# Masks of ones and zeros only: a bias product without its correction, w_in converted behind it, and a new order of the experts' blocks

## The chip, the cores and the metric

One Trainium2 chip, one of its cores. The metric is device time in microseconds (us); lower is better. The engines are TensorE (PE, with PEld for its weight loads), VectorE (DVE), ScalarE (ACT), GpSimd (POOL) and SyncE (SP), which issues most transfers.

## The reference, cut to what matters

Three stages over B=2, H=8, S=576, D=64 (1152 tokens, model width 512). Attention adds a bias that a small network with 32 hidden units makes from the distance of two positions:

```python
scores = q @ k.T / sqrt(D)
psi_rel = log1p(abs(pos_i - pos_j)); psi_i = log1p(max(pos_i, 1))
h = maximum((psi_rel / psi_i) * w1 + b1, 0)      # 32 hidden units
scores = scores + h @ w2                         # one bias per head
x = softmax(scores) @ v                          # 1152 x 512
h = x @ w_in                                     # 512 -> 1024
x = layernorm(h * softmax(h)) * g_ln @ w_out     # 1024 -> 512
# 8 experts, two per token, chosen by noisy logits and weighted by a softmax of the two
out[tokens of e] += weight * (maximum(x @ w1[e], 0) @ w2[e])
```

Each hidden unit of the bias network is zero below some distance and linear above it, or the reverse. So the bias of a row is a sum over units of (mask times slope times log distance) plus (mask times intercept), where the mask says whether the unit is on.

## The kernel before, in words

All of the kernel is in one program for one core, traced in program order by `_build`. The framework then gives every engine its own queue. Program order acts as a priority there: an instruction that is ready may be put ahead of one that stands before it in the program, unless it is held with `keep_in_program_order`. Each engine works its queue in order. In the trace the first absolute value of a w_in chunk (L260) runs on ScalarE at 31.02 us, while attention, whose loop traces it at step k = 20, begins at 48.6 us. Tiles come from pools with a fixed number of buffers; a writer waits until the last reader of the buffer is done.

**Bias.** The 576 query positions are worked in 18 tiles `mk` (m = 0 to 17) of 32 rows, each in two halves gg of 16 rows. `masks` (L183 to L194) makes the masks of one tile: 8 instructions of 128x576 in bf16, one for 4 query positions (32 units each on 128 partitions), with 3 buffers. `engine` (L178) says which engine makes which: the letters of MASK_ENG0 for m = 0, MASK_ENG1 for m = 1 to 6, MASK_ENG2 for m from 7 on. VectorE (D) and GpSimd (P) compare the distance with a threshold and write 1 or 0 (L194); ScalarE (A) writes the sign, 1 or -1 (L192).

`mix` (L196 to L219) is the product for one half: slope (`sl`) and intercept (`ic`) go to two PSUM tiles `d`, each in two bank halves of 288 columns. The four mask instructions u of the half are multiplied with 32 columns of weights each, into 32 partitions of PSUM each (L212). The weights are split into two fp16 parts, so each u takes two matmuls with `WD`. A mask of signs takes four: two with half the weights, `WH`, on the signs, and two with `WH` on a tile of ones, since (sign + 1)/2 is the mask. L216 and L217 on VectorE join slope, log distance and intercept; SP writes the rows to DRAM (`biasd`, L219), and `bias_in` (L232) reads them back as `bt`, per attention tile.

`bias_step(s)` (L221) traces four masks of tile m+1 and one `mix`. Steps 0 to 11 are traced ahead of attention, the other 24 one by one beside attention's steps k = 0 to 23.

**Attention.** 40 steps (5 query tiles `it`, 4 head pairs `hp`, 2 batches `b`), plus a tail. In step k the loop at L384 traces: transfers of later bias and q; every second step the value product `av` (L351) of the pair before; the transposes `tr` (L329) of the step two back; the scores `qk` (L302); and one bias step. `qk` adds bias to scores and takes the minimum of the negative in one VectorE instruction (L319); ScalarE takes the exponential (L326). `tr` transposes on TensorE; ScalarE copies four blocks (L341), VectorE the fifth (L343); GpSimd spreads the reciprocals of the sums (`rb`, L349) for `av`, whose result VectorE copies (L373) and multiplies (L374). The transposes, the two score tiles of a step and the two tiles of `mix` share three PSUM tiles `d` (L99).

**w_in and w_out** arrive as 64-bit floats; `f64_parts` (L253) rebuilds fp32 from the words and splits it in two parts hi and lo: absolute value on ScalarE (L260), a maximum on the engine that CI or CO names (L261), three bit operations on VectorE (L263 to L265), hi on ScalarE (L266), lo on GpSimd (L267). w_in comes in 8 chunks, started at the steps in CONV and cut into pieces for the following steps as CUTS says; three raw buffers (RB64), two buffers for the work (TB). The parts go into freed `mk` and `t` buffers. w_out's 8 chunks follow through the same buffers, while the second stage runs (L446 to L512).

**Experts** (L803 to L829). For each expert e: first products, 8 columns blocks f over 320 slots in three passes (L810), then ScalarE writes hT's first part (L812) and a copy of the last 64 slots, hL (L813), and VectorE the second part (L814), all from one PSUM tile. Second products (`second`, L781) run over slot blocks n = 0, 1 (128 slots, three passes over the split weights) and n = 2 (64 slots, fp32 on the raw weights `w2raw`, of which there are 4 buffers, one expert's worth). After n = 0 the loads of the next expert's w1 are traced; after n = 0 and n = 1 half of the next expert's transposes each (TK). `wload` (L659) loads raw weights and splits them on ScalarE and VectorE (L408, L409). Results are scattered with an add in DRAM (L644).

## Time and profile before

| | us |
|---|---|
| median of 3 runs (lowest to highest) | 672.72 (670.83 to 675.07) |
| the profiled execution | 674.53 |
| its span on the core | 672.70 |
| TensorE busy in the span | 610.1 (91%) |
| VectorE, ScalarE, GpSimd busy | 400.1, 329.7, 224.8 |
| mean granted TensorE clock | 0.975 of full speed |

The span runs from the first to the last instruction on the core; the execution's own time has 1.8 us around it. A busy TensorE is not TensorE at its peak, since matmuls are pipelined and their ends are modelled. The clock is either 1.2 or 2.4 GHz; a mean between 0.5 and 1 says how long a stretch spent at either. By stages: masks and bias alone to about 48 us, attention with the bias to about 200, attention alone to about 263, the second stage to 390, routing to 405, the experts to 660, and a tail of scatters.

### The profile page before, as it was taken

The numbers are of one execution on the slowest core, as the hardware profiler recorded it, in microseconds if no ns is written. First come the engines' busy times: TensorE is split into PE (matmuls) and PEld (weight loads), VectorE is DVE, ScalarE is ACT, GpSimd is POOL, SyncE is SP. The second block draws the span as 40 slices with busy tenths as digits, with TensorE's granted clock in tenths as the row PEclk, the third lists the DMA queues.
The fourth block names the chain that finished last, engine by engine and source line by source line (L and its number), as shares of the span: only waits on it lengthen the run. The fifth ranks groups of instructions, "written<-read, shape, count | busy, mean of one in ns | idle before, by whom it ended". The sixth has DMA issues, their size and how long they took to land. (4 is left out here: it accounts for less than half of the span.)

```text
span 672.7 us, 13660 instructions
## 1 busy us (share of the span) xinstructions
PE 610.1 (91%) x5516; PEld 503.0 (75%) x5516; DVE 400.1 (59%) x930; ACT 329.7 (49%) x637; POOL 224.8 (33%) x177
## 2 busy tenths in 40 slices
PE   0988999999877999989999989989999999999992
PEld 0766777777655788767888879788888888888781
DVE  3686767675667653896445797563828272635410
ACT  5644556555445665655334645353636353543410
POOL 5688665746235003631000301121212222122101
PEclk9988999999788999999999999999999999899997
DMA  8665521512634102400030406656575757361612
GB/s 321 197 239 218 196 86 37 211 68 76 236 130 147 50 2 104 168 32 32 32 141 16 157 18 219 191 162 188 156 220 149 241 147 199 112 165 49 164 18 27
DMA packets 33944, 89.48 MB, mean 133 GB/s; under 512 B 3600, under 2 KB 5136, under 8 KB 33872
## 3 DMA queue, kind: packets, MB, share of 16 engines
q1 hardware_dynamic: 26480, 72.04, 30.7%
q0 software_dynamic: 5808, 13.37, 9.4%
q10 hardware_dynamic: 1584, 3.11, 1.3%
q8 instruction: 45, 0.74, 0.5%
q14 instruction: 27, 0.22, 0.1%
HBM read 67.66 MB, written 20.84 MB: 132 GB/s over the span
## 5 line engine op out<-in xcount | busy, mean ns | idle before, releaser
L810 PE MATMUL phe<-xgt,wp 128*128 128x320 f32 x768 | 118.8, 314 | 9.8 <-DVE hT L814 7.6
L810 PEld LDWEIGHTS phe<-xgt,wp 128*128 128x128 f32 x768 | 114.2, 190 | 13.8 <-DVE hT L814 8.7
L194 POOL TENSOR_SCALAR mk<-T,thr 128x576 bf16<-128x576 f16 x56 | 97.9, 1761 | 45.5 <-PE d L212 34.1
L793 PE MATMUL poe<-wp,hT 128*128 128x512 f32 x384 | 90.5, 392 | 0.0
L644 POOL DMA_INDIRECT out<-y,si x24 | 38.0, 1585 | 152.2 <-ACT y L800 95.7
L793 PEld LDWEIGHTS poe<-wp,hT 128*128 128x128 f32 x384 | 71.2, 188 | 14.2
L212 PE MATMUL d<-mk,wd 128*32 128x288 bf16 x704 | 55.8, 298 | 25.8 <-POOL wd L171 15.7
L326 ACT ACTIVATE e<-e,nm 128x576 f32<-128x576 f32 x72 | 55.3, 769 | 47.7 <-DVE nm L319 47.7
L212 PEld LDWEIGHTS <-wh 128*32 128x32 f16 x896 | 56.9, 100 | 25.0 <-issue 10.6
L319 DVE CUSTOM_DVE_ANT_0 e<-d,bt 128x576 f32<-128x576 f32 x72 | 52.0, 755 | 32.1 <-PE d L310 24.5
L212 PE MATMUL d<-mk,wh 128*32 128x288 bf16 x448 | 64.0, 302 | 3.8 <-DVE nm L319 1.9
L409 DVE TENSOR_TENSOR wp<-w2raw,wp 128x1024 fp32r<-128x1024 f32 x32 | 39.2, 1224 | 45.8 <-ACT wp L408 45.1
L212 PE MATMUL d<-one,wh 128*32 128x288 bf16 x448 | 63.4, 299 | 0.0
L341 ACT ACTIVATE et<-d 128x1024 f32<-128x1024 f32 (+1 forms) x40 | 37.3, 935 | 38.1 <-PE d L338 38.1
L800 ACT ACTIVATE y<-poe,sw 128x512 f32<-128x512 f32 (+1 forms) x24 | 14.8, 618 | 83.8 <-issue 44.8
L212 PEld LDWEIGHTS <-wd 128*32 128x32 f16 x704 | 30.5, 96 | 28.2 <-POOL wd L171 15.7
L310 PE MATMUL d<-kv,q 64*128 64x288 f32 x256 | 46.1, 453 | 4.2 <-DVE nm L319 4.2
L812 ACT ACTIVATE hT<-phe 128x320 fp32r<-128x320 f32 x64 | 27.8, 434 | 39.3 <-PE phe L810 39.3
L192 ACT ACTIVATE mk<-T,thr 128x576 bf16<-128x576 f16 x56 | 38.9, 762 | 14.7 <-DVE t L217 6.4
L370 PE MATMUL av<-et,kv 128*64 128x128 f32 (+1 forms) x800 | 44.7, 267 | 0.0
L672 POOL DMA_INDIRECT xg<-x1d,gi x21 | 21.0, 998 | 70.1 <-DVE sf L633 32.8
L408 ACT ACTIVATE wp<-w2raw 128x1024 fp32r<-128x1024 f32 x32 | 33.9, 1060 | 19.4 <-DMA w2raw<-moe_w 19.4
(197 smaller groups left out, 1111.4 us busy)
## 6 DMA issues: line engine op xcount, KB each, us to landing
wraw<-moe_w SPq DMA_DIRECT2D x32, 512.0 KB, 4.5
w2raw<-moe_w SPq DMA_DIRECT2D x32, 512.0 KB, 6.5
biasd<-t SPq DMA_DIRECT2D x18, 576.0 KB, 3.1
bt<-biasd SPq DMA_DIRECT2D x16, 576.0 KB, 5.9
kv<-kv SPq DMA_DIRECT2D x8, 608.0 KB, 10.2
raw<-w_in SPq DMA_DIRECT2D x8, 512.0 KB, 5.2
raw<-w_out SPq DMA_DIRECT2D x8, 512.0 KB, 3.8
q<-q SPq DMA_DIRECT2D x5, 512.0 KB, 3.7
```

Of the source, the lines that this page charges most:

```text
L192: nc.scalar.activation(dst, w, AF.Sign, bias=thr[:, 1, q:q + 1])
L194: (V if e == "D" else P_).tensor_scalar(dst, w, thr[:, 0, q:q + 1], None, op0=OP.is_gt)
L212: nc.tensor.matmul(ps[32 * u:32 * u + 32, half, 0:288], l[n][0][:, 32 * a:32 * a + 32], l[n][1], start=(n == 0), stop=(n == len(l) - 1))
L310: nc.tensor.matmul(ss[x][:, a, 0:288], Q[it][h, n], k[h, a * 288:a * 288 + 288], start=True, stop=True)
L319: V.tensor_tensor_reduce(out=e.rearrange("p (a b) -> p a b", a=2), in0=ps[:, :, 0:288], in1=BT[it, hp][:, x].rearrange("p (a b) -> p a b", ...
L326: nc.scalar.activation(e, e, AF.Exp, bias=nm, scale=-1.0, accum_out=u.sums[:, c + x:c + x + 1])
L341: nc.scalar.activation(u.et[:, n * b:n * b + n, 0:4], pt[:, 0:n], AF.Copy)
L370: nc.tensor.matmul(o[64 * x:64 * x + 64, 0, b, 0:n], v[:, jb, 64 * x:64 * x + 64], w, start=(jb == 0), stop=(jb == JB - 1))
L409: return a, V.tensor_tensor(out=lo, in0=src, in1=hi.bitcast(F32), op=OP.subtract)
L644: nc.gpsimd.indirect_dma_start(out=dst, out_offset=bass.IndirectOffsetOnAxis(ap=si, axis=0), in_=y, in_offset=None, compute_op=OP.add, bou ...
L793: nc.tensor.matmul(po, hT[f][wh][:, j:j + R], W2[f // 2][ww_][:, c:c + N], start=(f == 0 and m == 0), stop=(f == 7 and m == 2))
L810: nc.tensor.matmul(ph[:, 0:CAP], w1[k][ww_][:, f * 128:f * 128 + 128], xt[wx][:, k], start=(k == 0 and n == 0), stop=(k == 3 and n == 2))
```

## The change

Every mask is now 1 or 0. ScalarE's come from a Sigmoid of (distance minus threshold) times 1e25, so `one`, `WH` and the two correcting matmuls per sign mask are gone; a table preload switches ScalarE back ahead of attention. From m = 7 on ScalarE makes no masks: of eight, GpSimd makes five and VectorE three (before: four, two, and two on ScalarE). ScalarE takes over two copies of attention, L343 and L373. `tr` is traced ahead of `av`. w_in's chunks are fetched from step 14 and converted from step 24, and the maximum runs on VectorE; q is loaded four steps later. Among the experts hL is written after hT's second part, and for all but the last expert the 64-slot block goes first, with loads and transposes at the same places in the order.

```diff
--- before.py
+++ after.py
@@ -41,7 +41,7 @@
 AB = 1
 SF = 3
 TK = {0: (0, 1), 1: (2, 3)}
-CONV = (20, 22, 24, 26, 28, 30, 32, 34)
+CONV = (24, 26, 28, 30, 32, 34, 36, 38)
 CUTS = (1, 1, 3, 1, 1)
 TR = 7
 FM = 2
@@ -49,7 +49,9 @@
 
 MASK_ENG0 = "DADADADA"
 MASK_ENG1 = "APAADAPA"
-MASK_ENG2 = "PAPDPAPD"
+MASK_ENG2 = "PDPPDPDP"
+
+STEP = 1e25
 
 
 
@@ -139,12 +141,10 @@
     V.tensor_tensor(out=arg, in0=arg, in1=thr[:, 1], op=OP.subtract)
     V.scalar_tensor_tensor(thr[:, 0], arg, 1.0, thr[:, 0], op0=OP.add, op1=OP.mult)
     V.tensor_scalar(thr[:, 0], thr[:, 0], -1.0, sg1[:, 3:4], op0=OP.add, op1=OP.mult)
-    V.tensor_scalar(thr[:, 1], thr[:, 0], -1.0, None, op0=OP.mult)
+    V.tensor_scalar(thr[:, 1], thr[:, 0], -STEP, None, op0=OP.mult)
     tc.keep_in_program_order(V.tensor_scalar(T, T, sg1[:, 3:4], None, op0=OP.mult))
 
     with tc.high_priority():
-        one = bp.tile([128, 288], BF, name="one")
-        P_.memset(one, 1.0)
         wab = bp.tile([128, 2, H], F32, name="wab")
         P_.tensor_scalar(wab[:, 0], w2c, w1c, 8.0, op0=OP.mult, op1=OP.mult)
         P_.tensor_scalar(wab[:, 1], w2c, b1c, 8.0, op0=OP.mult, op1=OP.mult)
@@ -165,14 +165,11 @@
         unscale = bp.tile([128, 1], F32, name="unscale")
         V.tensor_scalar(unscale, am[:, 2:3], 2.0 ** -9, None, op0=OP.mult)
         P_.tensor_scalar(W, W, am[:, 3:4], 2.0 ** 9, op0=OP.mult, op1=OP.mult)
-
-        WD, WH = ([bp.tile([128, 64], F16, name=f"{n}{k}") for k in range(2)] for n in ("wd", "wh"))
+        WD = [bp.tile([128, 64], F16, name=f"wd{k}") for k in range(2)]
         rest = bp.tile([128, 64], F32, name="rest")
         P_.tensor_copy(WD[0], W)
         P_.tensor_tensor(out=rest, in0=W, in1=WD[0], op=OP.subtract)
         P_.tensor_copy(WD[1], rest)
-        for k in range(2):
-            P_.tensor_scalar(WH[k], WD[k], 0.5, None, op0=OP.mult)
         V.tensor_scalar(inv, inv, unscale, None, op0=OP.mult)
 
     def engine(m, u):
@@ -189,7 +186,7 @@
             w = T[:, 572 - 4 * q:1148 - 4 * q]
             e = engine(m, u)
             if e == "A":
-                nc.scalar.activation(dst, w, AF.Sign, bias=thr[:, 1, q:q + 1])
+                nc.scalar.activation(dst, w, AF.Sigmoid, bias=thr[:, 1, q:q + 1], scale=STEP)
             else:
                 (V if e == "D" else P_).tensor_scalar(dst, w, thr[:, 0, q:q + 1], None, op0=OP.is_gt)
 
@@ -201,16 +198,11 @@
         sl, ic = dbank(), dbank()
         for a, ps in enumerate((sl, ic)):
             for half in range(2):
-                todo = []
-                for u in range(4):
-                    x = mk[:, 4 * gg + u, half * 288:half * 288 + 288]
-                    w = WH if engine(m, 4 * gg + u) == "A" else WD
-                    todo.append([(w[n], x) for n in range(2)] + [(w[n], one) for n in range(2) if w is WH])
-                for n in range(4):
-                    for u, l in enumerate(todo):
-                        if n < len(l):
-                            nc.tensor.matmul(ps[32 * u:32 * u + 32, half, 0:288], l[n][0][:, 32 * a:32 * a + 32], l[n][1],
-                                             start=(n == 0), stop=(n == len(l) - 1))
+                for n in range(2):
+                    for u in range(4):
+                        nc.tensor.matmul(ps[32 * u:32 * u + 32, half, 0:288], WD[n][:, 32 * a:32 * a + 32],
+                                         mk[:, 4 * gg + u, half * 288:half * 288 + 288],
+                                         start=(n == 0), stop=(n == 1))
         th = TT[m][:, gg].rearrange("p (a b) -> p a b", a=2)
         Lw = L[:, 560 - 16 * G:560 - 16 * G + S].rearrange("p (a b) -> p a b", a=2)
         V.scalar_tensor_tensor(th, Lw, inv[:, G:G + 1], sl[:, :, 0:288], op0=OP.mult, op1=OP.mult)
@@ -266,7 +258,7 @@
                 lambda: nc.scalar.activation(hi, tf, AF.Copy),
                 lambda: eng2.tensor_tensor(out=lo, in0=tf, in1=hi.bitcast(F32), op=OP.subtract))
 
-    CI = (P_, P_)
+    CI = (V, P_)
     CO = [(P_, P_)] * 4 + [(V, P_)] * 4
     WI = {}
 
@@ -340,7 +332,7 @@
             nc.tensor.transpose(u.rest[:, n * b + x], e[:, S - 128:S], ident)
         nc.scalar.activation(u.et[:, n * b:n * b + n, 0:4], pt[:, 0:n], AF.Copy)
         if b == 1:
-            V.tensor_copy(u.et[:, 0:2 * n, 4], u.rest[:, 0:2 * n])
+            nc.scalar.activation(u.et[:, 0:2 * n, 4], u.rest[:, 0:2 * n], AF.Copy)
             u.rs = ap.tile([128, 4], F32, name="rs", bufs=3)
             V.tensor_scalar(u.rs[:, 0:2 * n], u.sums[:, 0:2 * n], 1e-9, None, op0=OP.add)
             V.reciprocal(u.rs[:, 0:2 * n], u.rs[:, 0:2 * n])
@@ -370,29 +362,31 @@
                     nc.tensor.matmul(o[64 * x:64 * x + 64, 0, b, 0:n], v[:, jb, 64 * x:64 * x + 64], w,
                                      start=(jb == 0), stop=(jb == JB - 1))
         dst = XA[:, it:it + 5:4, hp] if n == 128 else XA[:, 8, hp].rearrange("p (b i) -> p b i", b=2)
-        V.tensor_copy(dst, o[:, 0, :, 0:n])
+        nc.scalar.activation(dst, o[:, 0, :, 0:n], AF.Copy)
         V.tensor_tensor(out=dst, in0=dst, in1=o[:, 1, :, 0:n], op=OP.mult)
 
     masks(0, 0, 8)
     for s in range(2 * PRE):
         bias_step(s)
+    tc.keep_in_program_order(nc.scalar.preload_act_table_set("natural_log_exp_and_others"))
     bias_in(0)
     bias_in(1)
     chunks = [(k, a) for k in range(4) for a in range(2)]
-    raws = [fetch_in(*c) for c in chunks[:RB64]]
-    conv = []
+    raws, conv = [], []
     for k in range(len(A) + LAG + 8):
         if k % 2 == 0 and k < len(A):
             bias_in(k // 2 + 2)
-        if k % 8 == 2 and k // 8 + 1 < 5:
+        if k % 8 == 6 and k // 8 + 1 < 5:
             load_q(k // 8 + 1)
+        if LAG <= k < len(A) + LAG:
+            tr(*A[k - LAG])
         if LAG <= k - 1 < len(A) + LAG and A[k - 1 - LAG][2] == 1:
             av(*A[k - 1 - LAG][:2])
-        if LAG <= k < len(A) + LAG:
-            tr(*A[k - LAG])
         if k < len(A):
             qk(*A[k])
         bias_step(2 * PRE + k)
+        if k == CONV[0] - 10:
+            raws = [fetch_in(*c) for c in chunks[:RB64]]
         if k in CONV:
             conv.append((list(conv_in(*chunks[0], raws.pop(0))), list(CUTS)))
             chunks.pop(0)
@@ -810,9 +804,9 @@
                     nc.tensor.matmul(ph[:, 0:CAP], w1[k][ww_][:, f * 128:f * 128 + 128], xt[wx][:, k],
                                      start=(k == 0 and n == 0), stop=(k == 3 and n == 2))
             nc.scalar.activation(hT[f][0], ph[:, 0:CAP], AF.Relu)
-            nc.scalar.activation(hL[:, f], ph[:, CAP - 64:CAP], AF.Relu)
             V.scalar_tensor_tensor(hT[f][1], ph[:, 0:CAP], 0.0, hT[f][0].bitcast(F32),
                                    op0=OP.max, op1=OP.subtract)
+            nc.scalar.activation(hL[:, f], ph[:, CAP - 64:CAP], AF.Relu)
             if e == 0 and f < 4:
                 W2.append(wload(w2s(e, f), ep, W2B, True, True))
             if e == 0 and f == SL0:
@@ -820,13 +814,14 @@
             if f == SF and e + 1 < E:
                 SI[e + 1] = slots(pm[:, :, e + 1], e + 1, SL, "")
                 xg = rows(SI[e + 1][0])
-        for n in range(NJ):
+
+        for i, n in enumerate((2, 0, 1) if e + 1 < E else range(NJ)):
             second(e, W2, n)
-            if n == 0 and e + 1 < E:
+            if i == 0 and e + 1 < E:
                 W1[e + 1] = [wload(w1s(e + 1, k), ea, WB) for k in range(4)]
                 XG[e + 1] = xgt()
-            if n in TK and e + 1 < E:
-                transposed(xg, XG[e + 1], TK[n])
+            if i in TK and e + 1 < E:
+                transposed(xg, XG[e + 1], TK[i])
 
 
     most = nc.values_load(cnt[0:1, E:E + 1], min_val=0, max_val=NT * 128,
```

## Rows read from the trace of the kernel before

**Rows 1.** Table of stages: stretch, length, busy us (instructions) by engine, granted clock, DMA.
```profile
15.70:48.00 32.30, 27.35 (x610) 21.62 (x612) 21.96 (x34) 19.24 (x29) 23.44 (x17) 0.95 0.64 219
...
100.00:150.00 50.00, 50.00 (x675) 38.30 (x675) 36.35 (x81) 27.73 (x51) 29.29 (x20) 1.00 0.29 107
150.00:198.00 48.00, 41.10 (x497) 30.87 (x489) 31.97 (x68) 23.14 (x43) 18.85 (x15) 0.89 0.40 137
198.00:264.00 66.00, 61.40 (x683) 49.02 (x682) 39.68 (x108) 40.19 (x80) 14.16 (x14) 0.97 0.22 72
264.00:300.00 36.00, 32.98 (x146) 25.03 (x145) 29.02 (x56) 19.34 (x36) 21.64 (x16) 1.00 0.36 126
```

**Rows 2.** Groups of L212 by shape: busy us, mean ns | idle before, releasers.
```profile
L212 PE MATMUL d<-mk,wh 128*32 128x288 bf16 x448 | 64.0, 302 | 3.8 <-DVE nm L319 1.9 <-POOL wh L175 1.7 <-DVE t L217 0.2
L212 PE MATMUL d<-one,wh 128*32 128x288 bf16 x448 | 63.4, 299 | 0.0
```

**Rows 3.** Timeline of TensorE beside attention: start us, length, line, count.
```profile
127.66 0.44 PE L361 MATMUL av<-ident,rb 128*128 128x128 f32 x2
...
132.77 0.30 PE L212 MATMUL d<-mk,wd 128*32 128x288 bf16 x1
...
134.84 1.09 PE L338 MATMUL d<-ident,e 128*128 128x128 f32 x8
...
136.08 1.24 PE L310 MATMUL d<-kv,q 64*128 64x288 f32 x8
137.25 0.30 PE L212 MATMUL d<-mk,wd 128*32 128x288 bf16 x1
...
139.32 0.44 PE L361 MATMUL av<-ident,rb 128*128 128x128 f32 x2
```

**Rows 4.** Timeline of SP, which issues the transfers, before attention.
```profile
28.77 0.38 SPq L219 DMA_DIRECT2D biasd<-t  x1
...
32.68 0.38 SPq L219 DMA_DIRECT2D biasd<-t  x1
```

**Rows 5.** Timeline of VectorE before attention.
```profile
36.63 0.43 DVE L263 TENSOR_SCALAR t<-t 128x512 uint32<-128x512 uint32 x1 [3.98 <-POOL t L261]
...
53.01 0.76 DVE L319 CUSTOM_DVE_ANT_0 e<-d,bt 128x576 f32<-128x576 f32 x1 [2.05 <-DMA bt<-biasd]
```

**Rows 6.** Timeline of GpSimd beside attention.
```profile
139.33 6.97 POOL L194 TENSOR_SCALAR mk<-T,thr 128x576 bf16<-128x576 f16 x4 [4.35 <-PE d L212]
146.25 0.39 POOL L349 COPY rb<-rs 128x256 f32<-128x256 f32 x1
```

**Rows 7.** Groups of ScalarE by shape.
```profile
L341 ACT ACTIVATE et<-d 128x512 f32<-128x512 f32 x8 | 4.7, 598 | 6.1 <-PE d L338 6.1
...
L78 ACT ACT_TABLE_LOAD x1 | 1.3, 1283 | 0.7 <-PEq L930 0.7
```

**Rows 8.** Timeline of VectorE beside attention.
```profile
138.04 0.76 DVE L319 CUSTOM_DVE_ANT_0 e<-d,bt 128x576 f32<-128x576 f32 x1
...
138.71 0.81 DVE L216 SCALAR_TENSOR_TENSOR t<-L,sp,d 128x576 f32<-128x576 f32 x1
139.44 0.80 DVE L194 TENSOR_SCALAR mk<-T,thr 128x576 bf16<-128x576 f16 x1
140.16 0.81 DVE L217 SCALAR_TENSOR_TENSOR t<-d,unscale,t 128x576 f32<-128x576 f32 x1
```

**Rows 9.** Timeline of TensorE at w_in's conversion.
```profile
172.61 0.40 PE L212 MATMUL d<-mk,wd 128*32 128x288 bf16 x1 [2.88 <-DVE nm L319]
...
190.54 0.28 PE L212 MATMUL d<-mk,wd 128*32 128x288 bf16 x1 [3.47 <-DVE nm L319]
```

**Rows 10.** Group of the experts' first products.
```profile
L810 PE MATMUL phe<-xgt,wp 128*128 128x320 f32 x768 | 118.8, 314 | 9.8 <-DVE hT L814 7.6 <-ACT xgt L408 2.3
```

**Rows 11.** Waits among the experts, 405 to 640 us: total, times, longest.
```profile
ACT wp L408 <- DMA w2raw<-moe_w: 19.4, 17, 2.5
```

**Rows 12.** Timeline of SP among the experts.
```profile
466.28 2.96 SPq L650 DMA_DIRECT2D w2raw<-moe_w  x4
```

## The prediction

> **What bounds the kernel now.** I read the table of stages first, then the groups of `mix`, then the timeline of one steady stretch engine by engine, and last the stalls. In the table [rows 1] TensorE is busy for all 50 us between 100 and 150, where attention and the bias run together: there it is the bound, with VectorE at 36, ScalarE at 28 and GpSimd at 29. Between 15.7 and 48 it is busy for 27 of 32, and between 150 and 198 only for 41 of 48, at a granted clock of 0.89. The groups of `mix` show what it does [rows 2]: 448 products with halved weights come with 448 more that multiply a tile of ones. Those serve only to turn ScalarE's signs into masks.
>
> The steady timeline gives the price [rows 3]. Two attention steps, one with the value product and one without, repeat every 11.66 us (127.66 to 139.32); one `mix` takes 132.77 to 134.84, 2.07 us. Its matmuls fill four column groups of 32 side by side, so what counts is the longest group: one with a ScalarE mask has four matmuls for each bank half, the others two. Every step has at least one such group.
>
> **The change, part by part.** I work against the profiled execution, 674.53 us; it lies 1.8 above the median of the runs, 672.72, so I take 1.8 off at the end. A measurement of this kernel can tell about 1% from no change.
>
> *One mask value.* Two rounds instead of four: 16 become 8 in a step, 2.07 becomes about 1.1, so 0.97 goes from each of 36 steps. That is 35 us of TensorE's work, 11.6 in the 12 steps before attention and 23.3 in the 24 beside it. How much of it comes out as time differs by stage.
>
> *Before attention.* The bias rows leave every 3.91 us (28.77 to 32.68 on SP's queue [rows 4]) until VectorE, which works in order, stops for 3.98 us for the maximum of a w_in chunk that GpSimd has not done; the first bias arrives at 53.01 [rows 5]. With the product halved, GpSimd is next late: two masks of 1.74 [rows 6] are 3.5 per mask tile, so six times 0.4, 2.5, goes. The maximum on VectorE takes away the stop, 4.0. Together 6.5. The bounds are 2.5, if w_in's work is still pulled ahead to this place and waits elsewhere, and 11.6, if all of TensorE's work comes out. Two activation table loads are added (one for Sigmoid, one back), 1.28 each by the only load in the trace [rows 7]; ScalarE idles 13 of 32 us here [rows 1], which hides them; uncovered they cost 2.6. Sigmoid masks I cost like the Sign masks; no row shows Sigmoid, so I bound it by the same 13 us of idle time: were each of the 34 a fifth longer, 5 us, it would still fit.
>
> The Trainium skill (ScalarE: Activation LUTs, "What ACT_TABLE_LOAD costs") adds a drain of about 1.4 us to each switch of sets, so by the page two switches would be 5.3 us instead of 2.6. No row here shows that drain. By that rule too the sum stays, as 5.3 fits in the idle 13.
>
> *Beside attention.* From TensorE alone a pair of steps would fall from 11.66 to 9.72. Then others come near. GpSimd gets five masks per pair instead of four: 5 x 1.74 + 0.39 for the spread of the reciprocals = 9.1 [rows 6]. VectorE gets one more mask and gives two copies to ScalarE. ScalarE loses two masks per pair and gets one copy of 128x512 and one of 128x256, at most 0.60 each [rows 7]; 40 such copies over all of attention are at most 24 us, beside idle time of 22 in every 50 [rows 1]. What I think decides is PSUM. Three tiles d go round five uses a step: transposes (freed by ScalarE), two score tiles (freed by the add-and-minimum, L319), and the two of `mix` (freed by L216 and L217). Counted from the end of the scores: the two L319 take a slot of 0.67 each and end at about 1.5; L216 and L217 of 0.73 each, with 0.81 for the last, and end at about 3.0 [rows 8]. The second score matmul of the next step needs the tile of L217, and scores take 1.17 (136.08 to 137.25) [rows 3]. So a step without the value product lasts 4.2, though TensorE needs only 4.48 - 0.97 = 3.5. The step with it (7.18 - 0.97 = 6.2) has 2.7 us of value product to cover the same chain. A pair is 10.4: 1.26 less, 15 us over 12 pairs. The bounds are 23 (9.72 a pair) and 4 (11.3 a pair, when a VectorE mask of up to 0.80 stands between L216 and L217, as at 139.44 [rows 8], and nothing of the value product fills the gaps).
>
> The Trainium skill (TensorEngine Tiling (Array Packing), "PSUM Bottleneck") warns that packing speeds up TensorE but not the emptying of PSUM. By that rule VectorE's chain sets the step, as in my 10.4 and more so in the rival below; by TensorE's rows alone it would be 9.72. The trace of before cannot decide it, as TensorE waits for nothing in its steady stretch.
>
> *w_in behind the bias, maximum on VectorE.* The stage from 150 to 198 holds the waits of w_in's conversion: TensorE idles 2.88 and 3.47 behind L319, which stands on VectorE behind a chunk [rows 9]. In all it idles 6.9 us, and a clock of 0.89 over 48 us means some 22% of it at the lower level, worth 5.3 more [rows 1]; so one such stall costs about 6.1. VectorE's wait for GpSimd's maximum goes; a wait for ScalarE's absolute value, and ScalarE's for GpSimd's subtraction, are late next. I take 5 of the 12, since part of the work still meets a full VectorE; bounds 0 and 12. The rest of the work then stands between 198 and 264 [rows 1], where VectorE and ScalarE have 26 us free each. Three bit operations back to back can be longer than VectorE's gap in the short step, some 0.4 in each of eight chunks, 3; against that, stops like those of rows 9 that reach into this stage go, 5. I take -2 (bounds -6, +3). w_out follows through the same three buffers; its conversion stands beside TensorE's work in 264 to 300, where TensorE idles 3 us [rows 1]: later by a chunk or two, I take +1.5 (0 to +5). On SP's queue w_in's fetches and q only move behind transfers that have to go first; I cost that at nothing, hidden by the steps between issue and use, with the same +5 as the end if that cover is gone.
>
> *Experts.* TensorE waits 7.6 us for hT in the first products, about 1.1 per expert after the first [rows 10], and ScalarE 19.4 for w2raw [rows 11]. The four w2 tiles are issued from 466.28 on [rows 12], only as the last block, the one of 64 slots, reads the raw tiles. With that block first they come free two blocks earlier, the transfers land under these, and the splits no longer bunch at the start of the first products. I take 5 of 7.6. hL behind L814 makes ScalarE wait for VectorE where VectorE waited before; the copy is short but in order, so this part is bounded at -7.6 and at +4, half as much again. The last expert keeps its order, so the end does not move.
>
> Sum: -6.5 - 15 - 5 - 2 + 1.5 - 5 = -32. 674.5 - 32 = 642.5, as a median 641.
>
> **Rivals.** *TensorE stays the bound: 9.72 a pair, the 12 us of stalls gone.* For it: instructions are put into gaps by a scheduler, and value products are ready. Then -6.5 - 23 - 12 - 2 + 1.5 - 5 = -47: 626. *Emptying PSUM becomes the bound: 11.3 a pair.* For it: VectorE has more masks, at the place where TensorE waits; against it, it gave two copies away. -6.5 - 4 - 5 - 2 + 1.5 - 5 = -21: 652. This is also what the skill's rule on packing would give.
>
> *Slower: GpSimd falls behind and the clock falls with it.* The place is the spread of the reciprocals, in order behind five masks; it ends 9.1 us into a pair of 10.4, where now it ends 4.3 us ahead of the value product (146.25 + 0.39 against 139.32 + 11.66) [rows 3, 6]. If it comes some 3 us late, a pair costs a stall of the 6.1 us kind. From six pairs of twelve on (37 against 32) the kernel is slower; with eight it is 642.5 + 49, as a median 690. Against it: 9.1 is below even 9.72, the transposes now stand ahead of the value product, 1.24 more, and a longer pair gives GpSimd time. *The change moves nothing*, because later stages put the time back: 11.3 a pair, no stall gone, and the later parts at their worst (+3, +5, +4) give -6.5 - 4 + 12, about +1: 674.
>
> **How the numbers follow.** The forecast 0.50, TensorE-bound 0.18, PSUM-bound 0.22, nothing 0.06, slower 0.04. From a little past the one fast rival to a little past the other, 622 to 660, lies 8 of 10. Faster by over 1% (below 666) 0.90, the three cases together; within 1% 0.06; slower 0.04.
>
> **What would show it.** Right: no group with ones in L212, a `mix` near 1.1 us, pairs of 10 to 11 us with small waits of TensorE for L319 or L217, the first bias in near 46 us, no idle time of VectorE behind GpSimd's maximum, w2raw issued during the second block, TensorE waiting under 3 us for hT. Wrong: pairs of 11.5 or more, GpSimd's spread as releaser of TensorE, a clock below 0.9 between 50 and 170 us, or new waits for w_in or w_out between 260 and 310.

## The result, and the profile after

The changed kernel takes 641.8 us (median of 4 runs, 641.1 to 642.0) beside 671.8 for the kernel before on the same chip: a ratio of 0.955, with a 95% interval of 0.950 to 0.960. The forecast was 641.0. In the last set of runs below, on another occasion, it took 639.9 beside 680.1, a ratio of 0.944 (0.939 to 0.950).

The profiled execution took 641.07 us (span 639.3; before 674.53 and 672.7). The two traces, cut at the same five events, show where the 33.4 us of the span come from:

| stretch, up to | before, us | after, us | difference | forecast |
|---|---|---|---|---|
| first add-and-minimum of attention | 53.01 | 42.05 | -11.0 | -6.5 |
| last product of the bias | 144.5 | 125.1 | -19.4 | -20 |
| first product of the second stage | 65.9 | 71.0 | +5.1 | -2 |
| first product of the experts | 141.5 | 141.2 | -0.3 | +1.5 |
| end | 267.8 | 260.0 | -7.8 | -5 |

The table of stages of the changed kernel, cut at its own events; the columns are those of [rows 1]:

```profile
14.25:42.00 27.75, 21.13 (x424) 12.97 (x424) 25.12 (x39) 20.54 (x30) 27.04 (x18) 0.96 0.81 296
90.00:140.00 50.00, 48.71 (x669) 37.03 (x669) 36.73 (x85) 28.73 (x56) 43.68 (x30) 1.00 0.32 119
140.00:167.00 27.00, 22.39 (x314) 16.84 (x314) 22.38 (x48) 17.77 (x35) 6.51 (x7) 1.00 0.53 191
```

Before attention TensorE is busy for only 21 of 27.75 us. GpSimd is busy for 27.04 and VectorE for 25.12, and TensorE's timeline tells which of the two it waits for:

```profile
33.63 1.39 PE L203 MATMUL d<-mk,wd 128*32 128x288 bf16 x32 [0.35 <-DVE t L209]
```

```profile
33.50 0.80 DVE L208 SCALAR_TENSOR_TENSOR t<-L,sp,d 128x576 f32<-128x576 f32 x1
...
35.24 0.80 DVE L208 SCALAR_TENSOR_TENSOR t<-L,sp,d 128x576 f32<-128x576 f32 x1
```

VectorE empties the product's tiles with L208 and L209 and makes a mask between them, without a pause, 1.74 us a step (33.50 to 35.24), and TensorE waits for it. GpSimd is full as well, but it works ahead: behind the first products TensorE waits for none of its masks. Beside attention TensorE has small gaps (48.71 of 50), where before it had none.

The groups with ones are gone, 1,152 products are left of 1,600; this is the group of `mix`, to be held against [rows 2]:

```profile
L203 PE MATMUL d<-mk,wd 128*32 128x288 bf16 x1152 | 48.7, 302 | 26.9 <-POOL wd L170 14.2 <-DVE nm L311 7.3 <-DVE t L209 2.5
```

TensorE's timeline over one pair of steps, as in [rows 3]:

```profile
105.56 0.68 PE L203 MATMUL d<-mk,wd 128*32 128x288 bf16 x16 [0.25 <-DVE nm L311]
...
107.48 1.64 PE L302 MATMUL d<-kv,q 64*128 64x288 f32 x8
109.05 1.19 PE L203 MATMUL d<-mk,wd 128*32 128x288 bf16 x32
110.25 1.09 PE L330 MATMUL d<-ident,e 128*128 128x128 f32 x8
...
116.13 0.67 PE L203 MATMUL d<-mk,wd 128*32 128x288 bf16 x16 [0.25 <-DVE nm L311]
```

The product is 1.20 (109.05 to 110.25) where it was 2.07. A pair is 10.57 (105.56 to 116.13) where it was 11.66; the forecast was 10.4. In the step with the value product the second half of the product waits 0.25 for the add-and-minimum to empty a tile. In the short step the scores take 1.64 instead of 1.24. That fits a wait inside the group for the tile that VectorE empties last:

```profile
107.01 0.82 DVE L209 SCALAR_TENSOR_TENSOR t<-d,unscale,t 128x576 f32<-128x576 f32 x1
```

VectorE before attention, against [rows 5]: the maximum L253 is now its own, and no stop behind GpSimd stands there.

```profile
38.76 0.41 DVE L253 TENSOR_SCALAR t<-t 128x512 f32<-128x512 f32 x1
...
42.05 0.76 DVE L311 CUSTOM_DVE_ANT_0 e<-d,bt 128x576 f32<-128x576 f32 x1 [0.43 <-DMA bt<-biasd]
```

TensorE at w_in's and w_out's conversion, against [rows 9], and in attention alone:

```profile
149.87 0.68 PE L203 MATMUL d<-mk,wd 128*32 128x288 bf16 x16 [2.25 <-DVE nm L311]
...
162.64 0.67 PE L203 MATMUL d<-mk,wd 128*32 128x288 bf16 x16 [1.84 <-DVE nm L311]
...
186.36 2.96 PE L302 MATMUL d<-kv,q 64*128 64x288 f32 x8 [2.19 <-DVE nm L311]
...
197.39 1.59 PE L302 MATMUL d<-kv,q 64*128 64x288 f32 x8
199.64 1.09 PE L330 MATMUL d<-ident,e 128*128 128x128 f32 x8 [0.66 <-ACT et L333]
```

The stops are shorter than the 2.88 and 3.47 of before, but not gone, and after the one at 186.36 the scores take 2.96 instead of 1.24, at the lower of the clock's two levels (granted: 0.91 between 170 and 190 us). That stop stands behind VectorE's wait for GpSimd's maximum of w_out:

```profile
183.87 0.83 DVE L255 TENSOR_SCALAR t<-t 128x512 uint32<-128x512 uint32 x1 [2.67 <-POOL t L253]
```

Something new stands at 199.64: the transposes wait 0.66 for ScalarE's copy `et`, in the two pairs that run without any conversion beside them. Such a pair is 8.45 (194.98 to 203.43).

Among the experts, the group of the first products, ScalarE's waits and SP's timeline answer to [rows 10 to 12]. TensorE's wait for hT is gone, ScalarE's for w2raw went from 19.4 to 5.7, and the four transfers leave while the 64-slot block, now the first, reads the raw tiles.

```profile
L804 PE MATMUL phe<-xgt,wp 128*128 128x320 f32 x768 | 115.9, 310 | 2.3 <-ACT xgt L402 2.3
```

```profile
ACT wp L402 <- DMA w2raw<-moe_w: 5.7, 6, 1.2
```

```profile
458.13 3.29 SPq L644 DMA_DIRECT2D w2raw<-moe_w  x4
```

### The profile page after: what moved, and what is told of

The parts are those of the page before. It is cut to its first block, busy times and chain, and to the rows that moved or that the text cites. A ratio compares the mean times of both kernels' runs of the same rounds, so it can differ in the third digit from the quotient of the medians.

```text
span 639.3 us, 12768 instructions
## 1 busy us (share of the span) xinstructions
PE 582.0 (91%) x5068; PEld 475.9 (74%) x5068; DVE 392.2 (61%) x909; ACT 341.9 (53%) x657; POOL 232.9 (36%) x177
## 3 DMA queue, kind: packets, MB, share of 16 engines
q10 hardware_dynamic: 1584, 3.11, 1.3%
## 5 line engine op out<-in xcount | busy, mean ns | idle before, releaser
L191 POOL TENSOR_SCALAR mk<-T,thr 128x576 bf16<-128x576 f16 x67 | 116.9, 1759 | 13.0 <-PE d L203 8.9
L804 PE MATMUL phe<-xgt,wp 128*128 128x320 f32 x768 | 115.9, 310 | 2.3 <-ACT xgt L402 2.3
L203 PE MATMUL d<-mk,wd 128*32 128x288 bf16 x1152 | 48.7, 302 | 26.9 <-POOL wd L170 14.2
L807 DVE SCALAR_TENSOR_TENSOR hT<-phe,hT 128x320 fp32r<-128x320 f32 x64 | 31.3, 489 | 50.2 <-ACT hT L806 49.7
L302 PE MATMUL d<-kv,q 64*128 64x288 f32 x256 | 51.0, 447 | 5.7 <-DVE nm L311 5.2
L362 PEld LDWEIGHTS av<-et,kv 128*64 128x64 f32 x800 | 41.0, 138 | 3.7 <-issue 3.3
L330 PE MATMUL d<-ident,e 128*128 128x128 f32 x288 | 40.8, 283 | 2.8 <-ACT et L333 1.7
L302 PEld LDWEIGHTS d<-kv,q 64*128 64x128 f32 x256 | 30.2, 193 | 17.2 <-DVE nm L311 6.9
L330 PEld LDWEIGHTS d<-ident,e 128*128 128x128 f32 x288 | 32.0, 143 | 13.4 <-DVE nm L311 7.8
L449 PE MATMUL ps<-mk,xs 128*128 128x512 f32 x162 | 40.5, 397 | 0.9 <-ACT xs L443 0.9
```

Of the source, the lines that this page charges most:

```text
L191: (V if e == "D" else P_).tensor_scalar(dst, w, thr[:, 0, q:q + 1], None, op0=OP.is_gt)
L203: nc.tensor.matmul(ps[32 * u:32 * u + 32, half, 0:288], WD[n][:, 32 * a:32 * a + 32], mk[:, 4 * gg + u, half * 288:half * 288 + 288], star ...
L302: nc.tensor.matmul(ss[x][:, a, 0:288], Q[it][h, n], k[h, a * 288:a * 288 + 288], start=True, stop=True)
L330: nc.tensor.transpose(pt[:, x, jb], e[:, jb * 128:jb * 128 + 128], ident)
L362: nc.tensor.matmul(o[64 * x:64 * x + 64, 0, b, 0:n], v[:, jb, 64 * x:64 * x + 64], w, start=(jb == 0), stop=(jb == JB - 1))
L449: nc.tensor.matmul(ph[:, a], xs[wx][:, k], WI[k, a][ww], start=(k == 0 and n == 0), stop=(k == 3 and n == 2))
```

## Experiments

Each edits the changed kernel. Stretches are those of the table above, taken in the same way; the changed kernel has 42.05, 125.1, 71.0, 141.2 and 260.0. The runs were made on three chips, on which the kernel before took 679 to 681 us in the median. The changed kernel itself was run again on one of them only (639.9), so on the others a difference of 2 us from 641.8 in the total shows nothing.

One reading holds for all of them. How long attention takes beside the bias and how long alone depends on the stop behind which the clock falls, and that is not the same in every run, even where nothing in attention was edited (see the experts below). The sum of both stretches moves less: 195.9 to 197.0 us in the five traces whose attention is the changed kernel's or differs only in the number in CONV. So the sum is given where a run moves both stretches.

**The rounds of the product.**

```
-                for n in range(2):
-                    for u in range(4):
-                        nc.tensor.matmul(ps[32 * u:32 * u + 32, half, 0:288], WD[n][:, 32 * a:32 * a + 32],
+                for n in range(4):
+                    for u in range(4) if n < 2 else (1,):
+                        w = WD[n] if n < 2 else WZ
+                        nc.tensor.matmul(ps[32 * u:32 * u + 32, half, 0:288], w[:, 32 * a:32 * a + 32],
...
```

WZ holds zeros.

> The changed kernel (641.8 us) with two more rounds of matmuls for one column group in every product of the bias, with weights of zero, so that the longest group has four matmuls again; masks and everything else stay. Theory (TensorE's rounds carry the gain of both stages): product from 1.1 to about 2.07 us, pairs of steps from 10.58 to 11.5 to 11.7, 12 to 13 us more beside attention and 6 to 11 before it: 658 to 666. Rival (emptying of PSUM sets the pace and hides the two rounds): pairs under 11, under 650 in all.

Measured: 654.2 us (652.3 to 655.2). Attention begins at 46.7 (+4.6) and the stretch beside it takes 135.7 (+10.6). TensorE's timeline of this kernel, the value product of two pairs in a row:

```profile
100.18 2.40 PE L365 MATMUL av<-et,kv 128*64 128x128 f32 x40
...
111.69 0.55 PE L365 MATMUL av<-et,kv 128*64 128x128 f32 x6
```

A pair is 11.51, with no wait in it. So the rounds are worth 0.94 a pair, and about 4.6 before attention. The total lies below the theory's 658 to 666 and above the rival's 650: the theory holds beside attention, and its "6 to 11" before attention was too high. There VectorE, not TensorE, sets the changed kernel's pace, which leaves room for a part of the rounds.

**What sets the pair of 10.57.**

```
 def masks(m, lo, hi):
+    if m > 6:
+        MK[m] = MK[6]
+        return
```

> The changed kernel (641.8 us) without the masks of the mask tiles 7 to 17: their products read mask tile 6 again, so the bias of most queries is left out. Theory (beside the bias the emptying of PSUM by VectorE sets the pair of 10.58 us, and the masks on GpSimd and VectorE stand beside it): pairs of 10.2 to 10.6 us. Rival (the masks set it, GpSimd's five of 1.74 or VectorE's between two additions): pairs of 9.7 to 9.8 us, TensorE's own sum, and some 10 us less in the stage.

Measured: 633.7 us in two runs (630.7 and 636.7). TensorE's timeline:

```profile
108.04 0.68 PE L206 MATMUL d<-mk,wd 128*32 128x288 bf16 x16 [0.25 <-DVE nm L314]
...
118.61 0.67 PE L206 MATMUL d<-mk,wd 128*32 128x288 bf16 x16 [0.25 <-DVE nm L314]
```

The pair is 10.57 without a single mask, with the same wait of 0.25 for the same add-and-minimum. Neither GpSimd's five masks nor VectorE's set the pace; the rival falls. The wait points to what is left, the way of a PSUM tile from TensorE through VectorE and back. Before attention GpSimd has far less to do here (17.8 us instead of 27), and attention begins at 40.1, only 1.9 earlier.

**The engine of the maximum.**

```
-    CI = (V, P_)
+    CI = (P_, P_)
```

> The changed kernel (641.8 us) with the maximum of w_in's chunks on GpSimd again, their place kept. Theory (VectorE stands still behind GpSimd's maximum, 1 to 1.5 us a chunk longer than now behind ScalarE's absolute value): the stops of TensorE between 140 and 190 us longer, the second stage begins 2 to 5 us later, 644 to 647. Rival (GpSimd is idle there, and one operation less on VectorE pays for the stop): 640 to 642.

Measured: 658.2 us (657.6 to 659.1), 16 more, far outside both. Attention begins at 54.7 (+12.6), later than in the kernel before; the stretch beside it takes 129.9 (+4.8). VectorE's and GpSimd's timelines of this kernel:

```profile
51.70 0.83 DVE L255 TENSOR_SCALAR t<-t 128x512 uint32<-128x512 uint32 x1 [13.28 <-POOL t L253]
```

```profile
16.96 33.24 POOL L191 TENSOR_SCALAR mk<-T,thr 128x576 bf16<-128x576 f16 x19
50.17 2.95 POOL L253 TENSOR_SCALAR t<-t 128x512 f32<-128x512 f32 x2
```

GpSimd now makes 19 masks without a pause, 33 us of them, and the maximum stands behind them in its queue. VectorE, in order too, waits 13.28 us for it, where it waited 3.98 before the change [rows 5]. Whether it is the larger share of masks or w_in's later fetch that puts so many masks ahead of the maximum was not tried apart.

**The place of w_in's conversion.**

```
-CONV = (24, 26, 28, 30, 32, 34, 36, 38)
+CONV = (20, 22, 24, 26, 28, 30, 32, 34)
```

> The changed kernel (641.8 us) with w_in's conversion four steps earlier again and its fetches with it, the maximum still on VectorE. Theory (with the maximum on VectorE the place matters little: the stops move four steps ahead into the steady stretch): last product of the bias 1 to 4 us later, attention alone as much shorter, 640 to 643. Rival (the place behind the bias is what saved the stops): 645 to 650, the second stage begins 3 us or more later.

Measured: 641.5 us (640.6 to 642.0), and all five stretches within 0.6 us of the changed kernel's. Nothing moved, which neither theory said. TensorE's timeline and ScalarE's, changed kernel first:

```profile
140.78 1.19 PE L203 MATMUL d<-mk,wd 128*32 128x288 bf16 x32
```

```profile
142.88 1.14 ACT L258 ACTIVATE mk<-t 128x512 fp32r<-128x512 f32 x2
```

```profile
143.17 1.14 ACT L258 ACTIVATE mk<-t 128x512 fp32r<-128x512 f32 x2
```

The high part of a chunk is written into a tile `mk` of the masks, and these have three buffers. The first one that w_in gets is that of mask tile 15, whose second product, the one at 140.78, has just ended. The buffer sets the place, not the number in CONV. The kernel before, too, writes its first high part behind the product of mask tile 15, at 163.07. And without masks from tile 7 on, in the run above, where buffers are free from the start, it is written at 46.57.

**The copies on ScalarE.**

```
-  nc.scalar.activation(u.et[:, 0:2 * n, 4], u.rest[:, 0:2 * n], AF.Copy)
+  V.tensor_copy(u.et[:, 0:2 * n, 4], u.rest[:, 0:2 * n])
...
-  nc.scalar.activation(dst, o[:, 0, :, 0:n], AF.Copy)
+  V.tensor_copy(dst, o[:, 0, :, 0:n])
```

> The changed kernel (641.8 us) with both copies of attention (the rest columns and the value product) back on VectorE. Theory (the copies on ScalarE cost 0.5 us a pair in attention alone, where ScalarE sets the pace, and save VectorE beside the bias): attention alone back from 8.45 to about 7.9 us a pair, 3 to 5 us less there; beside the bias a pair of 10.58 becomes 10.6 to 11.2, up to 7 us more over 12 pairs; in all 638 to 645. Rival 1 (ScalarE has room everywhere, and the 8.45 comes from something else): pairs stay at 8.45 in attention alone, time unchanged or longer. Rival 2 (VectorE is full beside the bias): pairs there near 11.6, time over 648.

Measured: 641.7 us (640.4 to 642.7). Beside attention 128.2 (+3.1), attention alone 68.6 (-2.4), together 196.8. TensorE's timeline:

```profile
105.71 0.67 PE L203 MATMUL d<-mk,wd 128*32 128x288 bf16 x16 [0.25 <-DVE nm L311]
...
116.29 0.67 PE L203 MATMUL d<-mk,wd 128*32 128x288 bf16 x16 [0.25 <-DVE nm L311]
...
201.52 1.09 PE L330 MATMUL d<-ident,e 128*128 128x128 f32 x8 [0.65 <-ACT et L333]
```

The steady pair stays at 10.58 with two more operations on VectorE, and the wait of 0.65 in attention alone stays too. The copies are not its cause: of the theory only the total was right. Nor is the shift between the stretches shown to be theirs, since a run with nothing edited in attention has the same (the experts, below). The copies are worth nothing on balance.

**The exchanged order in a step.**

```
+        if LAG <= k - 1 < len(A) + LAG and A[k - 1 - LAG][2] == 1:
+            av(*A[k - 1 - LAG][:2])
         if LAG <= k < len(A) + LAG:
             tr(*A[k - LAG])
-        if LAG <= k - 1 < len(A) + LAG and A[k - 1 - LAG][2] == 1:
-            av(*A[k - 1 - LAG][:2])
```

> The changed kernel (641.8 us) with the value product ahead of the transposes in a step again, as before the change. Without both copies on ScalarE the pair in attention alone stayed at 8.45 us, with the same wait of 0.65 for ScalarE's copy of the transposes. Theory (the exchanged order makes that wait, since scores follow the transposes with nothing between): pairs in attention alone back to 7.9, 2 to 4.5 us less there; beside the bias 10.4 to 11.2 a pair (the chain of PSUM loses its cover in the short step, or not), 0 to 7 us more. Rival (the order is harmless, the pair of 8.45 comes from the later conversion of w_in): pairs stay at 8.45.

Measured: 641.2 us (638.7 to 643.1). Attention alone takes 65.8 (-5.2), the stretch beside the bias 130.1 (+5.0), together 195.9. TensorE's timeline in attention alone:

```profile
199.93 1.59 PE L302 MATMUL d<-kv,q 64*128 64x288 f32 x8
...
204.15 1.09 PE L330 MATMUL d<-ident,e 128*128 128x128 f32 x8
```

A pair is 7.88 (199.93 to 207.81, from these scores to those of the next pair), and the wait for `et` is gone from such pairs. ScalarE's timelines tell why, the changed kernel first, then this one:

```profile
198.59 1.00 ACT L333 ACTIVATE et<-d 128x1024 f32<-128x1024 f32 x1
```

```profile
201.12 1.00 ACT L333 ACTIVATE et<-d 128x1024 f32<-128x1024 f32 x1
```

In both, `et` comes behind two exponentials and empties its tile at 199.59 and 202.12. In the changed kernel only one set of scores stands between that and the next transposes, and TensorE is through with them at 198.98; here the value product stands there as well, and they start at 204.15. So the order is the cause of the 8.45. It is not shown to be the cause of the 5 us that the stretches exchange. The two pairs without conversion give 1.1 of the 5.2, and beside the bias the steady pair is only 0.07 longer (10.65 here). Much of the rest is the clock, which falls at w_in's conversion here and does not in the changed kernel (first row; this run's is the second):

```profile
150.00:160.00 10.00, 9.50 (x126) 7.36 (x118) 7.96 (x18) 8.13 (x16) 3.08 (x3) 1.00 0.84 323
```

```profile
150.00:160.00 10.00, 8.26 (x100) 6.06 (x93) 7.87 (x18) 5.72 (x12) 0.30 (x1) 0.83 0.76 289
```

Over both stretches the order gains nothing (195.9 beside 196.1).

**The maximum of w_out.**

```
-    CO = [(P_, P_)] * 4 + [(V, P_)] * 4
+    CO = [(V, P_)] * 8
```

> The changed kernel (641.8 us) with the maximum of the first four chunks of w_out on VectorE instead of GpSimd. Theory (VectorE's stop of 2.67 us behind GpSimd's maximum in attention alone costs 2.2 us of TensorE's time and, with the half clock after it, 5 in all): 636 to 639, no half clock between 186 and 195 us. Rival (the stop is caused by something else, or other work takes its place): 641 to 643.

Measured: 643.3 us (641.5 to 645.4), outside both ranges. The stop at 186 is gone, the granted clock stays at 1.00, and attention alone takes 66.9 (-4.0, together 191.9), as the theory has it; but the second stage takes 145.4 (+4.2). The tables of stages in ten-microsecond steps, of the changed kernel and of this one:

```profile
260.00:270.00 10.00, 8.64 (x40) 6.05 (x39) 9.56 (x20) 5.12 (x11) 4.25 (x3) 1.00 0.15 52
```

```profile
250.00:260.00 10.00, 9.10 (x46) 6.90 (x46) 10.00 (x25) 6.13 (x14) 3.35 (x3) 1.00 0.16 54
260.00:270.00 10.00, 6.87 (x26) 4.16 (x25) 9.27 (x16) 3.88 (x7) 4.50 (x4) 1.00 0.00 0
```

VectorE (third engine) is full where w_out's later chunks are converted, and more work there makes TensorE (first) wait: 6.87 of 10 from 260 on. (The second stage begins 4.5 us earlier in this run, so its rows lie that much deeper in the stage; the rows of like depth, not shown, differ in the same way, 8.51 and 6.99.) The gain was given back one stage later.

**Attention alone put right.** The order of before and VectorE's copies from the last product of the bias on, and w_out's maximum as in the run above:

> The changed kernel (641.8 us) with three edits: after the last product of the bias the value product stands ahead of the transposes and both copies are on VectorE again (beside the bias as changed), and the maximum of w_out's first chunks is on VectorE. Theory (the 4.9 us that attention alone lost come from these): 634 to 637, the stage after the last product of the bias 64 to 66 us instead of 70.9. Rival (the later place of w_in's conversion costs it): 69 to 71 in that stage, 640 to 642.

Measured: 640.3 us (639.2 to 643.3). Attention alone takes 64.5, inside the theory's 64 to 66, together 189.4. TensorE idles 2.5 us there instead of 6.5. So these edits give back more than the 5 us, 4.2 by the maximum and 2.5 by order and copies (in the sums), without touching the later place; but the second stage takes 145.3 again, and the total misses the 634 to 637.

**The experts.**

```
-        for i, n in enumerate((2, 0, 1) if e + 1 < E else range(NJ)):
+        for i, n in enumerate(range(NJ)):
```

> The changed kernel (641.8 us) with the experts' blocks back in the order 0, 1, 2 and nothing else undone. Theory (w2's raw tiles come free two blocks earlier with the 64-slot block first, and that is the 7.8 us that the experts' stage gained): 648 to 650, ScalarE's wait for w2raw back from 5.7 to about 19 us, TensorE's wait for hT back near 7. Rival (the gain comes from moving hL behind VectorE's part): within 1 us of 641.8.

Measured: 649.1 us (644.7 to 651.2), the experts 268.1 (+8.1). Waits among them:

```profile
ACT wp L402 <- DMA w2raw<-moe_w: 21.9, 13, 3.4
...
PE phe L804 <- ACT hL L809: 5.9, 5, 1.9
```

This run leaves attention as it is, and yet the stretch beside the bias took 128.4 (+3.3) and attention alone 68.6 (-2.3). Its stops are as long as the changed kernel's, but the clock falls behind others:

```profile
149.96 0.67 PE L203 MATMUL d<-mk,wd 128*32 128x288 bf16 x16 [2.24 <-DVE nm L311]
...
189.52 1.91 PE L302 MATMUL d<-kv,q 64*128 64x288 f32 x8 [2.22 <-DVE nm L311]
```

```profile
150.00:160.00 10.00, 9.39 (x112) 7.23 (x113) 6.82 (x15) 7.28 (x14) 1.85 (x2) 0.83 0.80 317
```

From 180 to 190 its clock is 1.00. In the changed kernel it is the reverse, 1.00 from 150 to 160 and 0.83 from 180 to 190.

The other half of the edit, with hL ahead of VectorE's operation again:

> The changed kernel (641.8 us) with hL back in front of VectorE's operation, the block order (2, 0, 1) kept. Theory (the block order carries the gain): 641 to 643. Rival (the place of hL carries it): 647 to 650, with TensorE's wait for hT back near 7 us.

Measured: 640.7 us (638.0 to 641.4), the experts 258.8 (-1.2), with no wait for hT. The block order carries the whole gain; the place of hL is worth nothing or a little less.

**A version that takes these together.** As in the run with attention alone put right, but only w_out's first two chunks have their maximum on VectorE, and hL is ahead again. With it ran the changed kernel itself.

> The changed kernel once more, unaltered, beside the kernels of this call. All theories: 640 to 644, first add-and-minimum at 42, last product of the bias at 167, first product of the second stage at 238, experts from 379.

> The changed kernel (641.8 us) with four edits: as before, after the last product of the bias the value product stands ahead of the transposes and both copies are on VectorE; w_out's maximum is on VectorE for the first two chunks alone (these are done in attention alone, where VectorE has room; with the first four there, attention alone was 6.5 us shorter and the second stage, where VectorE is full, 4.2 us longer); hL ahead of VectorE's operation. Theory (the second stage gets its 4.2 back): 634 to 637, attention alone 64 to 65 us, from there to the experts 141 to 142. Rival (an earlier start of the second stage is always lost to w_out's parts): that stretch 144 to 146, 638 to 641.

Measured: 636.1 us (635.1 to 638.5, six runs) beside 639.9 (639.1 to 644.6, six runs) for the changed kernel; against the kernel before, 0.938 (0.934 to 0.943) and 0.944 (0.939 to 0.950). All six runs lie below all six of the changed kernel, by 0.6% in the medians. Attention alone takes 64.7, the second stage 142.0: the theory holds. This version is faster than the kernel before and, by a small margin that no run contradicts, than the changed kernel.

## Why the prediction was right, and where it was not

**The total** was right to 1 us, and that is in part luck. The two stretches of attention were forecast at -22 together and came to -14.3; the three others were forecast at -10 and came to -19.1. The errors cancel.

**Before attention**, forecast -6.5, measured -11.0, near the bound of 11.6. The prediction had GpSimd next late, at 3.5 a mask tile. The pace came out, but by luck: VectorE sets it, at 1.74 a step, and no mask of GpSimd's is waited for. The sum had six times 0.4 for the halved product; the rounds give 4.6. It had no term for the start. TensorE's timeline of the kernel before:

```profile
15.68 0.66 PE L212 MATMUL d<-mk,wd 128*32 128x288 bf16 x2 [15.68 <-POOL wd L171]
18.02 0.42 PE L212 MATMUL d<-mk,wh 128*32 128x288 bf16 x1 [1.69 <-POOL wh L175]
```

The first product comes 1.4 earlier, at 14.25, and the wait of 1.69 for the halved weights is gone. That leaves 3.3 for the stop (forecast 4.0), as a remainder. And the terms don't simply add: with GpSimd's maximum kept, the change gains nothing here (54.7 beside 53.01). The new work on GpSimd and the maximum off GpSimd belong together; the prediction cost them apart.

**Beside attention**, forecast -20, measured -19.4. The step "three tiles d, emptied by VectorE" held: 10.57 a pair, 13.1 over twelve, and it holds without masks. One wait shows a tile earlier than forecast, at the product's second half; the forecast one, of the scores for VectorE's last tile, fits the 1.64 of the short step. The Trainium skill (TensorEngine Tiling (Array Packing), "PSUM Bottleneck") was right in direction, that emptying PSUM bounds a packed product; the pair it would have given in the prediction, 11.3, did not come. The rival with TensorE at 9.72 falls as well. The remaining 6.3 lie at w_in's stops (forecast 5), but these shortened by only 1.8: with the small ones beside them they are 5.1 us instead of 6.9. Most of the rest is the clock, 1.00 between 140 and 167 where it was 0.89 [rows 1]. That it did not fall there is not the change's sure doing: in the run with the old block order it did, and the stretch took 3.3 us more. What was named as late next came: VectorE waits some 1.7 us for ScalarE's absolute value in three places, and TensorE 2.25, 1.84 and 1.22 behind that.

**Attention alone** is the step that failed: "I take -2 (bounds -6, +3)", measured +5.1. The prediction gave this term to the later place of w_in's conversion, but the place did not move at all. It named the exchanged order of transposes and value product only for the time that it gives GpSimd, and did not ask what the value product had covered: ScalarE's exponentials and `et`. That costs 0.57 in each of the two pairs without conversion. Over the whole stretch:

```profile
197.81:263.39 65.58, 60.98 (x680) 48.63 (x680) 39.37 (x107) 39.77 (x79) 13.84 (x13) 0.97 0.23 74
```

```profile
167.44:238.13 70.69, 64.17 (x681) 51.21 (x681) 34.72 (x95) 45.86 (x98) 10.66 (x13) 0.95 0.24 78
```

TensorE idles 6.5 us where it idled 4.6, and 1.3 of that difference is the wait for `et`. The larger part, 3.2, is that as many matmuls take longer, where the clock is at its lower level behind the stop for w_out's maximum. That maximum stayed on GpSimd, and taking it away gave back 4.0. How much of this the change caused stays open, since the kernel before has a stop of the same kind there (3.11 at 207.76, behind w_in's maximum), and since the clock falls elsewhere in the run with the old block order.

**Second stage and experts.** +1.5 (bounds 0 and +5) against -0.3 measured: the later conversion of w_out cost nothing that shows. -5 against -7.8, a little past the bound of -7.6: the wait for hT went whole, and the four us feared from hL did not come.

**GpSimd behind, slower** did not come: behind the spread of the reciprocals and one more mask it still idles 1.58 us in each pair (119.42 to 121.00). The two table loads cost nothing that shows:

```profile
7.09 0.32 ACT L138 ACTIVATE thr<-thr 128x144 f32<-128x144 f32 x1
7.43 1.28 ACT L189 ACT_TABLE_LOAD   x1
9.31 22.96 ACT L189 ACTIVATE mk<-T,thr 128x576 bf16<-128x576 f16 x34 [0.60 <-DVE T L145]
32.29 1.28 ACT L371 ACT_TABLE_LOAD   x1
```

The drain of about 1.4 us that the Trainium skill adds (ScalarE: Activation LUTs, "What ACT_TABLE_LOAD costs") does not show in this trace. At the first load there is no room for all of it: the operation before ends at 7.41, the one behind starts at 9.31, so the whole switch takes at most 1.90, less than the half of the prediction's 5.3, and its idle 0.60 ends with the wait for T. Here the measurement decides: this switch cost less than the page's sum. Behind the second load ScalarE waits for w_in's transfer until 37.87, which would hide it.

## What to carry to other kernels

When work moves onto an engine, look for what already stands in that engine's queue and is waited for by another in-order engine: here the changed kernel keeps its gain before attention only with the maximum off GpSimd. When the order of two operations is exchanged, ask what the one had covered, in every stage that uses the order. Before giving a difference between two neighbouring stages to an edit, look at the granted clock in both and at a run that edits neither: here 2 to 3 us moved from one to the other with no edit in either. Before giving a saving to a place in the order, check whether that place or a buffer decides when the work runs.

## What was not expected of the hardware

Stops of like length had different ends: after 2.25 us at 149.87 the product ran at full speed (0.68), after 2.19 us at 186.36 the scores took 2.96 instead of 1.24, and the transposes behind them 1.91 instead of 1.09. What tells the two apart was not tried; in the run with the old block order, with the same code in attention, it was the other way round (2.24 at 149.96 and 2.22 at 189.52). In the last set of runs the kernel before spread over 672.5 to 684.4 us in eleven runs, the changed kernel over 639.1 to 644.6 in six; why the former spreads more stays open.
